# Gelu written back into its PSUM bank and split from there by VectorE, chunk 0's B and C as float32 rows, and the high weights' products first, in a fused scan and two-layer kernel

## The chip, the core and the metric

The kernel runs on one core of a Trainium2 chip. The metric is device time in microseconds (us) of one execution; a run is compared by the median of its executions. The engines have short names here: PE is TensorE, DVE is VectorE, ACT is ScalarE, POOL is GpSimd, and SP is the engine whose queue issues most DMAs.

## What is computed

Three stages stand behind one another. A chunked state-space scan over 768 positions gives y for 4 batches and 8 heads; y, as 3072 rows of 256, goes through two feed-forward layers of width 2048, the first with a sigmoid form of gelu, the second with a clipped form of swish.

```python
cum = np.cumsum(la, axis=-1)                                # la = log(clip(a))
L = np.exp(cum[:, :, :, None] - cum[:, :, None, :]) * causal
CB = np.einsum('bhin,bhjn->bhij', Cc, Bc)
y_intra = np.einsum('bhij,bhjd->bhid', CB * L, xc)
y_inter = np.einsum('bhin,bhnd->bhid', Cc, state) * np.exp(cum)[:, :, :, None]
y[:, :, sl] = y_intra + y_inter                             # and a new state for the next chunk
...
h = x @ w_in;  g = h * (1.0 / (1.0 + np.exp(-1.702 * h)));  x = g @ w_out          # first layer
h = x @ w_in;  g = h * np.clip(h + 3.0, 0.0, 6.0) / 6.0;    out = g @ w_out        # second layer
```

## The kernel before

**Scan.** The 768 positions are cut into 8 chunks c of 96, and each chunk has 4 batches b; the pair is a number q = 4c + b, 0 to 31. For each q and each half g of the heads, `decay` (L374, DVE) makes the decay matrix l by a scan instruction, `s_mm` (L446 for chunk 0, L455 for the others, PE) the products of B and C in a PSUM bank, and their product is the tile gm: by `g_mul` (L458, DVE), or for six of them by a copy on ACT (L461) and `g_pool` (L465, POOL). `y_mm` (L476, PE) multiplies gm by x; `y_out` (L484, ACT) and `y_lo` (L489, DVE) split the result into a high and a low part, the tile xt that the first layer reads. For chunks of q up to 3 the decay row is spread by PE (`a_spread`, L364); later ones load it by DMA (`a_load`).

**Layers.** The 3072 rows are cut into 7 blocks of 384 or 480 columns (`WID`). A unit is one block k, one layer (kind A or B) and one of 16 slices m of the width of 2048: 224 units. A unit is six matmuls of `l1` (L627) into one of two PSUM banks h, the activation, and six of `l2` (L663) into two banks acc. Each factor is a sum of a high and a low part (wh and wl, xt, gh and gl), and the three larger of four products are taken. In a unit of kind A, ACT runs gelu twice out of the bank (L636: to gg in SBUF, and to gh, which rounds), and `g_lo` (L649) on POOL makes gl = gg - gh. In a unit of kind B, ACT, DVE (`hard`, L645) and ACT (L640) make gg and gh, and POOL makes gl.

**Weights.** 32 weight tiles p (16 for each layer) arrive as 64-bit words, 512 KB each, in three buffers raw. Each is decoded: `w_scale` (L293, ACT) into one of two buffers dec, `w_low` (L298, DVE), `w_join` (L302, DVE), `w_top` (L305, ACT) to wh, and `w_bottom` (L311) to wl, on POOL for p under 16 and on DVE from 16 on. The last 9 tiles wl share memory with a tile `late`, which chunk 0's B and C (bcz and cbd) use first.

**Order.** Everything is added to a list with a due time (`key`), an assumed duration, and what it reads and writes; a planner (`Schedule.run`) walks the list with these durations and writes one order for each engine. The engines then run their order strictly, each instruction waiting for semaphores. The order of units is written out: block 0 alone for `LEAD` = 14 slices, then the rest of block 0 between slices of block 1, and so on.

For chunk 0, C is laid out as a block-diagonal tile: `c_block` multiplies it by a mask for each of 8 heads, on ACT (five) and POOL (three), and `s_mm` then makes one matmul of 128 x 448 for each q and g. Chunks 1 to 3 (`ROWS`) use 16 partition rows of float32 for each head instead, and eight matmuls of 16 x 112 for each q.

Of the kernel before, what the change touches and what calls it, by code (L numbers as in the profile page):

```python
# [36 lines left out]
LEAD = 14  # L37
# [5 lines left out]
LOWP = lambda p: False  # L43
TOPA = lambda p: True
# [163 lines left out]
def ssd_moe_kernel(ctx: ExitStack, tc: tile.TileContext, xs, aa, bc, bcz_d, bc0, wu, pat, idn, out):  # L208
# [4 lines left out]
    add = sch.add  # L213

# [19 lines left out]
    bcz = late[:, 0:2 * NB * E].rearrange("p (s b e) -> p s b e", s=2, b=NB)  # L234
    cbd = late[:, 2 * NB * E:10 * NB * E].rearrange("p (h b e) -> p h b e", h=NH, b=NB)
# [36 lines left out]
    mm = lambda k: max(0.1733, WID[k] / 2400 + 0.0025)  # L272
# [31 lines left out]
    def w_top(p, act):  # L304
        (nc.scalar.copy if act else nc.vector.tensor_copy)(w_hi[p], B_(f"dec:{p}").bitcast(F32))  # L305
# [472 lines left out]
```

## Time and profile before

| | |
|---|---|
| runs | median 622.89 us of 3 (621.64 to 623.63) |
| the profiled execution | 621.37 us, of it a span of 619.6 us from first to last instruction |
| busy share of the span | PE 97%, ACT 49%, POOL 53%, DVE 44% |
| granted TensorE clock | 0.993 over the span |
| first matmul of the layers | 23.54 us after the span's start |

The profiled execution is 1.5 us under the median of the runs. The parts of the prediction are worked out inside the profiled execution. A busy share is a mean over the whole span; the stretches differ.

### The profile page before, as it was taken

How to read it: one execution, taken by the hardware profiler on the slowest of the kernel's cores; microseconds unless marked ns; L12 is line 12 of the kernel's file. 1: busy time of each engine (PE TensorE's matmuls, PEld its weight loads, DVE VectorE, ACT ScalarE, POOL GpSimd, SP SyncE). 2: the span in 40 equal slices, each digit the busy share in tenths (PEclk: the TensorE clock that was granted, in tenths of full speed). 3: DMA queues.
4: the chain of work that ended last, by engine and by line, in shares of the span. 5: the costliest groups of instructions: out<-in, count | busy, mean ns of one | idle time of the engine just before them, and what ended most of it. 6: DMA issues, size and time to landing. Idle time of an engine off the chain costs nothing.

```text
span 619.6 us, 9459 instructions
## 1 busy us (share of the span) xinstructions
PE 600.7 (97%) x3580; PEld 527.5 (85%) x3580; DVE 273.6 (44%) x370; ACT 303.9 (49%) x629; POOL 327.3 (53%) x275
## 2 busy tenths in 40 slices
PE   9697799999999999999999999999999999999997
PEld 6575698889999899888888888888888899988997
DVE  6799996655751665412533414523103210032222
ACT  5555665566554454434544336444335444454453
POOL 5699984345475553434843447443344445444452
PEclk9799999999999999999999999999999999999999
DMA  4966553335113492340604404403000000000000
GB/s 145 248 189 197 166 196 109 119 110 175 50 52 107 122 264 78 90 138 1 169 2 129 129 2 122 139 1 118 0 2 1 0 17 15 2 1 1 33 0 27
DMA packets 45918, 53.69 MB, mean 87 GB/s; under 512 B 26176, under 2 KB 37296, under 8 KB 45872
## 3 DMA queue, kind: packets, MB, share of 16 engines
q1 hardware_dynamic: 45600, 52.97, 29.2%
q8 instruction: 28, 0.46, 0.3%
q14 instruction: 18, 0.15, 0.1%
q10 hardware_dynamic: 272, 0.12, 0.1%
HBM read 42.01 MB, written 10.60 MB: 85 GB/s over the span
## 4 chain that ended last, share of the span: by engine, by line
PE 89%; DVE 7%; DMA 1%; issue 1%; ACT 1%; POOL 0%; ACTq 0%; DVEq 0%; POOLq 0%; SPq 0%
PE h L627 43%; PE acc L663 42%; DVE l L374 3%; PE s L455 2%; DVE dec L302 2%; DVE raw L298 1%; PE y L476 1%; DVE gm L458 1%; PE s L476 1%; DMA raw<-in_wu 1%; DMA pat_sb<-in_pat 1%; PE acc L455 0%; DVE xt L489 0%; POOL wl L311 0%; ACT dec L293 0%
## 5 line engine op out<-in xcount | busy, mean ns | idle before, releaser
L649 POOL TENSOR_TENSOR gl<-gg,gh 128x384 fp32r<-128x384 f32 (+1 forms) x223 | 270.3, 1215 | 269.8 <-ACT gh L640 120.1
L627 PE MATMUL h<-xt,wh 128*128 128x480 f32 (+1 forms) x896 | 290.6, 367 | 2.1 <-DVE xt L489 1.8
L627 PEld LDWEIGHTS h<-xt,wh 128*128 128x128 f32 x896 | 168.2, 189 | 21.1 <-issue 2.2
L645 DVE SCALAR_TENSOR_TENSOR gg<-gg,h 128x480 f32<-128x480 f32 (+1 forms) x112 | 68.3, 610 | 229.2 <-ACT gg L638 228.9
L663 PE MATMUL acc<-gh,wh 128*128 128x384 f32 (+1 forms) x448 | 161.8, 361 | 0.0
L663 PE MATMUL acc<-gl,wh 128*128 128x384 f32 (+1 forms) x448 | 128.1, 362 | 0.0
L627 PE MATMUL h<-xt,wl 128*128 128x480 f32 (+1 forms) x322 | 117.8, 366 | 5.9 <-POOL wl L311 5.9
L663 PE MATMUL acc<-gh,wl 128*128 128x480 f32 (+1 forms) x322 | 117.9, 366 | 0.0
L636 ACT ACTIVATE gg<-h 128x480 f32<-128x480 f32 (+1 forms) x112 | 59.9, 537 | 111.2 <-PE h L627 102.8
L638 ACT ACTIVATE gg<-h 128x480 f32<-128x480 f32 (+1 forms) x112 | 60.2, 538 | 78.4 <-PE h L627 72.6
L640 ACT CAST gh<-gg 128x480 fp32r<-128x480 f32 (+1 forms) x112 | 62.6, 559 | 66.1 <-DVE gg L645 66.0
L663 PEld LDWEIGHTS acc<-gh,wh 128*128 128x128 f32 x448 | 84.1, 188 | 7.0
L663 PEld LDWEIGHTS acc<-gl,wh 128*128 128x128 f32 x448 | 82.8, 188 | 8.5 <-POOL gl L649 0.4
L374 DVE TENSOR_TENSOR_SCAN l<-l,pat_sb 112x448 f32<-112x448 f32 x56 | 80.4, 1462 | 5.5 <-DMA l<-acl_d 5.4
L627 PEld LDWEIGHTS h<-xt,wl 128*128 128x128 f32 x322 | 61.2, 190 | 12.4 <-POOL wl L311 7.6
L663 PEld LDWEIGHTS acc<-gh,wl 128*128 128x128 f32 x322 | 60.4, 188 | 7.4 <-issue 2.1
L636 ACT ACTIVATE gh<-h 128x480 fp32r<-128x480 f32 (+1 forms) x112 | 59.7, 533 | 11.5 <-PE h L627 11.5
L663 PE MATMUL acc<-gh,w_late 128*128 128x480 f32 (+1 forms) x126 | 45.8, 364 | 0.0
L627 PE MATMUL h<-xt,w_late 128*128 128x480 f32 (+1 forms) x126 | 45.6, 362 | 0.0
L458 DVE TENSOR_TENSOR gm<-s,l 112x448 f32<-112x448 f32 x28 | 17.3, 618 | 45.5 <-PE s L455 38.2
L302 DVE SCALAR_TENSOR_TENSOR dec<-dec,raw 128x512 uint32<-128x512 uint32 x32 | 33.6, 1049 | 2.4 <-ACT dec L293 0.3
L305 ACT CAST wh<-dec 128x512 fp32r<-128x512 f32 x32 | 19.8, 621 | 20.8 <-DVE dec L302 20.7
(60 smaller groups left out, 384.2 us busy)
## 6 DMA issues: line engine op xcount, KB each, us to landing
raw<-in_wu SPq DMA_DIRECT2D x32, 512.0 KB, 4.8
l<-acl_d SPq DMA_DIRECT2D x28, 392.0 KB, 4.8
st<-scr SPq DMA_DIRECT2D x8, 896.0 KB, 5.5
scr<-tsplit SPq DMA_DIRECT2D x32, 168.0 KB, 3.0
xs<-in_xs SPq DMA_DIRECT2D x8, 384.0 KB, 6.1
out<-gg SPq DMA_DIRECT2D x10, 192.0 KB, 2.0
scr<-tsplit SPq DMA_DIRECT2D x16, 112.0 KB, 2.2
raw<-in_bc SPq DMA_DIRECT2D x4, 384.0 KB, 5.5
```

Of the source, the lines that this page charges most:

```text
L302: nc.vector.scalar_tensor_tensor(t, t, 3, B_(f"raw:{p}")[:, :, 0], ALU.logical_shift_left, ALU.bitwise_or)
L305: (nc.scalar.copy if act else nc.vector.tensor_copy)(w_hi[p], B_(f"dec:{p}").bitcast(F32))
L374: nc.vector.tensor_tensor_scan(t, a, pat_sb, 0.0, ALU.mult, ALU.add)
L455: nc.tensor.matmul(out=ps[:, k, :], lhsT=l, rhs=r, start=True, stop=True)
L458: nc.vector.tensor_tensor(out=B_(f"gm:{q}.{g}"), in0=s_bank(q, g), in1=B_(f"l:{q}")[:, 4 * g:4 * g + 4], op=ALU.mult)
L627: nc.tensor.matmul(out=ps, lhsT=w[p][:, 128 * j:128 * j + 128], rhs=x[:, xp, j, 0:n], start=(i == 0), stop=(i == 5))
L636: nc.scalar.activation(g, ps, AF.Gelu_apprx_sigmoid)
L638: nc.scalar.activation(g, ps, AF.Relu, bias=3.0)
L640: nc.scalar.copy(g, B_(f"gg:{u}")[:, 0:n])
L645: nc.vector.scalar_tensor_tensor(out=g, in0=g, scalar=6.0, in1=B_(f"h:{u}")[:, 0:n], op0=ALU.min, op1=ALU.mult)
L649: e.tensor_tensor(out=B_(f"gl:{u}")[:, 0:n], in0=B_(f"gg:{u}")[:, 0:n], in1=B_(f"gh:{u}")[:, 0:n].bitcast(F32), op=ALU.subtract)
L663: nc.tensor.matmul(out=acc[d], lhsT=w[p][:, 256 + 128 * d:384 + 128 * d], rhs=g, start=(m == 0 and d not in seen), stop=(m == NM - 1 and d ...
```

## The change

- **Gelu.** In units of kind A, ACT writes gelu back into the PSUM bank h, then copies the bank to gh, and DVE makes gl out of the bank and gh. POOL has `g_lo` only for kind B. (`GLV` is now true for all units.)
- **Weights.** `w_bottom` runs on POOL for all 32 tiles.
- **Chunk 0.** `ROWS` now has chunk 0 too: B and C come as rows of float32 by eight DMAs of 56 KB, four of them on ACT's queue, and `c_block` is gone. The rows of chunks 0 to 2 lie in two buffers inside `late`, which also holds a fourth buffer for l (for q = 3).
- **The first DMAs.** The clipped decay factors (acl) take a buffer gg and no longer one of the three raw; pat is issued ahead of idn.
- **Order of products.** `l1` is two pieces: four matmuls with wh, and then two with wl, which alone wait for wl.
- **Planner.** `LEAD` is 12, the assumed durations are new, and an operation on DVE marked `port` is lengthened where it overlaps one on POOL, and the reverse.

```diff
-LEAD = 14
+LEAD = 12
-BOTV = lambda p: p >= 16
-GLV = lambda u, n: u == n - 1
+BOT = lambda p: "POOL"
+GLV = lambda u: True
-CBE = ["ACT", "ACT", "ACT", "POOL", "ACT", "POOL", "ACT", "POOL"]
-ROWS = (1, 2, 3)
+ROWS = (0, 1, 2, 3)
...
+            if o["port"]:
+                other = "DVE" if e == "POOL" else "POOL"
+                o["dur"] += (0.45 if e == "POOL" else 0.6) * max(0.0, min(port[other] - t, o["dur"]))
+                port[e] = t + o["dur"]
...
-    bcz = late[:, 0:2 * NB * E].rearrange("p (s b e) -> p s b e", s=2, b=NB)
-    cbd = late[:, 2 * NB * E:10 * NB * E].rearrange("p (h b e) -> p h b e", h=NH, b=NB)
+    r16_b = [late[:, 16 * E * i:16 * E * i + 16 * E] for i in range(2)]
+    lx_b = [late[0:E, 32 * E:40 * E].rearrange("p (h e) -> p h e", h=NH)]
...
-    add("ACT", 0.1, -90, consts, 0, w=["idn"], kb=20)
-    add("ACT", 0.1, -90, consts, 1, w=["pat"], kb=100)
+    add("ACT", 0.1, -91, consts, 1, w=["pat"], kb=100)
+    add("ACT", 0.1, -90, consts, 0, w=["idn"], kb=20, after=0.05)
...
-    add("SP", 0.4, -80, a_all, new=["raw:acl"], kb=115)
+    add("SP", 0.4, -80, a_all, new=["gg:acl"], kb=115)
...
+        elif c == 0:
+            src = bcz_d[s][64 * g:64 * g + 64].rearrange("(k n) (j p) e -> n p j k e", k=4, p=2)[:, i // 2]
+            eng.dma_start(out=t[:, s].rearrange("n (j k) e -> n j k e", j=2), in_=src)
...
-    def l1(u):
+    def l1(u, lo):
...
-        seq = [(w_hi, 1, 0), (w_lo, 0, 0), (w_hi, 1, 1), (w_lo, 0, 1), (w_hi, 0, 0), (w_hi, 0, 1)]
+        for w, xp, j in ((w_lo, 0, 0), (w_lo, 0, 1)) if lo else ((w_hi, 1, 0), (w_hi, 1, 1), (w_hi, 0, 0), (w_hi, 0, 1)):
...
+        elif kind == "A" and part == 0:
+            nc.scalar.activation(ps, ps, AF.Gelu_apprx_sigmoid)
...
+            nc.scalar.copy(B_(f"gh:{u}")[:, 0:n], ps if kind == "A" else B_(f"gg:{u}")[:, 0:n])
...
+        g = B_(f"{'h' if order[u][0] == 'A' and GLV(u) else 'gg'}:{u}")[:, 0:n]
+        e.tensor_tensor(out=B_(f"gl:{u}")[:, 0:n], in0=g, in1=B_(f"gh:{u}")[:, 0:n].bitcast(F32),
...
+        add("PE", 4 * mm(k), t, l1, u, False, r=W[:1] + [xname(kind, k)] + parts[kind, k], new=[f"h:{u}"])
+        add("PE", 2 * mm(k), t - 50, l1, u, True, r=W[1:] + [xname(kind, k)], w=[f"h:{u}"])
```

What stands in DVE's order when block 0 begins, before the change (raw and dec are weight tiles, l a decay matrix, gm its product with the bank s or acc):

```order
L298 TENSOR_SCALAR raw0_129<-raw0_129 128x512
L302 SCALAR_TENSOR_TENSOR dec1_133<-dec1_133,raw0_129 128x512
L374 SCALAR_TENSOR_TENSOR l1_135<-l1_135,pat_sb_68 112x448 x2
L298 TENSOR_SCALAR raw2_131<-raw2_131 128x512
L302 SCALAR_TENSOR_TENSOR dec0_132<-dec0_132,raw2_131 128x512
L298 TENSOR_SCALAR raw1_130<-raw1_130 128x512
L302 SCALAR_TENSOR_TENSOR dec1_133<-dec1_133,raw1_130 128x512
L374 SCALAR_TENSOR_TENSOR l2_136<-l2_136,pat_sb_68 112x448 x2
```

and after it, at the same place (L387 is now `decay`, L305 `w_low`, L309 `w_join`, L640 `g_lo`):

```order
L387 SCALAR_TENSOR_TENSOR l0_134<-l0_134,pat_sb_68 112x448
L305 TENSOR_SCALAR raw2_131<-raw2_131 128x512
L309 SCALAR_TENSOR_TENSOR dec0_132<-dec0_132,raw2_131 128x512
L640 TENSOR_TENSOR gl0_152<-h1_159,gh0_149 128x384
L305 TENSOR_SCALAR raw0_129<-raw0_129 128x512
L309 SCALAR_TENSOR_TENSOR dec1_133<-dec1_133,raw0_129 128x512
L640 TENSOR_TENSOR gl1_153<-h0_158,gh1_150 128x384
L387 SCALAR_TENSOR_TENSOR l0_134<-l0_134,pat_sb_68 112x448
L387 SCALAR_TENSOR_TENSOR l1_135<-l1_135,pat_sb_68 112x448
```

One `g_lo` now stands behind each join, and reads the bank h; before, none stood on DVE here. On POOL, the same stretch held one tile wl and one gl by turns before the change:

```order
L311 TENSOR_TENSOR wl2_107<-dec0_132,wh2_75 128x512
L649 TENSOR_TENSOR gl0_152<-gg0_147,gh0_149 128x384
L311 TENSOR_TENSOR wl3_108<-dec1_133,wh3_76 128x512
L649 TENSOR_TENSOR gl1_153<-gg1_148,gh1_150 128x384
L649 TENSOR_TENSOR gl2_154<-gg0_147,gh2_151 128x384
L311 TENSOR_TENSOR wl4_109<-dec0_132,wh4_77 128x512
```

and holds tiles wl alone after it, with a product gm for the scan (L468) here and there:

```order
L318 TENSOR_TENSOR wl2_107<-dec0_132,wh2_75 128x512
L318 TENSOR_TENSOR wl3_108<-dec1_133,wh3_76 128x512
L318 TENSOR_TENSOR wl4_109<-dec0_132,wh4_77 128x512
L468 TENSOR_TENSOR gm1_138<-gm1_138,l0_134 112x448
L318 TENSOR_TENSOR wl5_110<-dec1_133,wh5_78 128x512
```

On SP, the queue of the first DMAs before the change, in which the third weight tile stands behind acl's store and takes a buffer that the first tile had:

```order
L383 DMA late_128<-in_bcz 128x448 x2
L377 DMA xs0_141<-in_xs 96x1024
L288 DMA raw1_130<-in_wu 128x1024
L288 DMA raw2_131<-in_wu 128x1024
L356 DMA acl_d_155<-raw0_129 128x224
L288 DMA raw1_130<-in_wu 128x1024
```

and after it, where the first three tiles have a buffer each:

```order
L433 DMA late_128<-in_bcz 16x8x112 x4
L390 DMA xs0_141<-in_xs 96x1024
L295 DMA raw0_129<-in_wu 128x1024
L367 DMA acl_d_155<-gg0_147 128x224
L295 DMA raw1_130<-in_wu 128x1024
L295 DMA raw2_131<-in_wu 128x1024
```

The third weight tile no longer waits for a buffer.

## Rows read from the trace of the kernel before

**Rows 1.** Busy time by stretch: engines' busy us (instructions), granted clock, DMA share, GB/s.

```profile
0.00:23.50 23.50, 18.06 (x124) 11.37 (x124) 17.21 (x25) 11.82 (x26) 13.45 (x19) 0.94 0.61 196
23.50:27.50 4.00, 3.96 (x12) 3.96 (x13) 2.55 (x4) 1.63 (x4) 1.34 (x2) 0.50 1.04 266
...
30.00:71.40 41.40, 32.30 (x256) 26.26 (x255) 40.32 (x40) 22.61 (x52) 38.10 (x26) 1.00 0.62 181
100.00:600.00 500.00, 499.70 (x2888) 441.71 (x2887) 182.96 (x266) 240.67 (x490) 242.97 (x210) 1.00 0.24 70
```

**Rows 2.** PE's waits from 0 to 80 us: who waited for whom, us, times, longest.

```profile
PE h L627 <- POOL wl L311: 5.9, 6, 1.4
```

**Rows 3.** The chain of waits: start us, us, what.

```profile
15.27 5.10 DMA raw<-in_wu
...
23.54 5.32 PE h L627 x18
...
590.08 2.10 PE h L627 x12
```

**Rows 4.** Timeline of DVE, 0 to 110 us: start us, us, instruction.

```profile
5.14 3.05 DVE L374 TENSOR_TENSOR_SCAN l<-acc,pat_sb 112x448 f32<-112x448 f32 x3 [1.86 <-DMA pat_sb<-in_pat]
...
18.14 1.08 DVE L374 TENSOR_TENSOR_SCAN l<-acc,pat_sb 112x448 f32<-112x448 f32 x1
...
45.73 0.42 DVE L298 TENSOR_SCALAR raw<-raw 128x512 uint32<-128x512 uint32 x1
46.25 0.69 DVE L302 SCALAR_TENSOR_TENSOR dec<-dec,raw 128x512 uint32<-128x512 uint32 x1
46.86 2.15 DVE L374 TENSOR_TENSOR_SCAN l<-l,pat_sb 112x448 f32<-112x448 f32 x1
...
49.45 0.34 DVE L489 TENSOR_TENSOR xt<-y,xt 128x192 fp32r<-128x192 f32 x1
...
66.26 1.78 DVE L302 SCALAR_TENSOR_TENSOR dec<-dec,raw 128x512 uint32<-128x512 uint32 x1
...
103.73 2.06 DVE L374 TENSOR_TENSOR_SCAN l<-l,pat_sb 112x448 f32<-112x448 f32 x2
```

**Rows 5.** Groups of instructions, 23.5 to 71.4 us: busy us, mean ns | idle before, releaser.

```profile
L311 POOL TENSOR_TENSOR wl<-dec,wh 128x512 fp32r<-128x512 f32 x12 | 20.4, 1698 | 4.9 <-ACT wh L305 4.9
L649 POOL TENSOR_TENSOR gl<-gg,gh 128x384 fp32r<-128x384 f32 x13 | 19.9, 1532 | 2.9 <-ACT gh L636 2.7 <-POOL wl L311 0.3
L374 DVE TENSOR_TENSOR_SCAN l<-l,pat_sb 112x448 f32<-112x448 f32 x10 | 17.8, 1794 | 1.3 <-DMA l<-acl_d 1.3
L302 DVE SCALAR_TENSOR_TENSOR dec<-dec,raw 128x512 uint32<-128x512 uint32 x12 | 17.2, 1429 | 1.4 <-ACT dec L293 0.3
L298 DVE TENSOR_SCALAR raw<-raw 128x512 uint32<-128x512 uint32 x12 | 7.2, 601 | 0.0
```

**Rows 6.** Timeline of POOL: start us, us, instruction.

```profile
14.44 1.74 POOL L465 TENSOR_TENSOR gm<-gm,l 112x448 f32<-112x448 f32 x1 [0.93 <-ACT gm L461]
...
54.91 1.26 POOL L311 TENSOR_TENSOR wl<-dec,wh 128x512 fp32r<-128x512 f32 x1
...
101.70 1.00 POOL L649 TENSOR_TENSOR gl<-gg,gh 128x384 fp32r<-128x384 f32 x1 [1.39 <-PE acc L663]
```

**Rows 7.** Groups by shape over the whole span, columns as in rows 5.

```profile
L636 ACT ACTIVATE gg<-h 128x384 f32<-128x384 f32 x48 | 23.5, 490 | 36.1 <-PE h L627 28.8 <-POOL gl L649 7.0 <-DMA out<-gg 0.3
L458 DVE TENSOR_TENSOR gm<-acc,l 112x448 f32<-112x448 f32 x16 | 9.8, 614 | 0.0
L671 DVE TENSOR_TENSOR xt<-acc,xt 128x384 fp32r<-128x384 f32 x6 | 3.1, 551 | 1.1 <-ACT xt L673 1.1
```

**Rows 8.** DMA issues: KB each, median us to landing.

```profile
raw<-in_wu SPq DMA_DIRECT2D x32, 512.0 KB, 4.8
...
st<-in_bc SPq DMA_DIRECT2D x32, 24.0 KB, 2.0
late<-in_bcz SPq DMA_DIRECT2D x2, 224.0 KB, 3.7
```

More of the change, by code (lines that the diff above doesn't have):

```diff
@@ L139, in run @@
         ends = {}
+        port = {"DVE": 0.0, "POOL": 0.0}
         pipe = 0.0
@@ L213, in ssd_moe_kernel @@
     add = sch.add
+    ENG = {"ACT": nc.scalar, "DVE": nc.vector, "POOL": nc.gpsimd}
     const = pool("const")
@@ L271, in ssd_moe_kernel @@
     NU = len(order)
[L272 removed]
+    mm = lambda k: 0.000452 * WID[k]
     tu, t = [], START
@@ L443, in s_mm @@
                 ps = s_bank(q, g)
-                if c == 0:
-                    if k == 0:
-                        nc.tensor.matmul(out=ps, lhsT=bcz[:, 0, b], rhs=cbd[:, 4 * g:4 * g + 4, b], start=True, stop=True)
-                    continue
                 if c in ROWS:
@@ L503, in ssd_moe_kernel @@
     sname, yname, rows = {}, {}, {}
-    add("SP", 0.4, -80, a_all, new=["raw:acl"], kb=115)
-    add("DVE", 0.35, -80, a_clip, w=["raw:acl"])
-    add("SP", 0.4, -70, bcz_load, 1, w=["bcz1"], kb=230)
-    add("SP", 0.4, -69, bcz_load, 0, w=["bcz0"], kb=230)
-    add("SP", 0.4, -1, a_store, r=["raw:acl"], w=["acl_d"], kb=115)
-    for h in range(NH):
-        e = CBE[h]
-        add(e, {"ACT": 0.55, "POOL": 0.95, "DVE": 0.4}[e], -50 + h, c_block, h, e, r=["bcz1", "idn"], w=[f"cbd{h}"])
+    add("SP", 0.4, -80, a_all, new=["gg:acl"], kb=115)
+    add("DVE", 0.35, -80, a_clip, w=["gg:acl"])
+    add("SP", 0.4, -1, a_store, r=["gg:acl"], w=["acl_d"], kb=115)
     add("POOL", 0.4, -40, zero_xs, new=["xs:0"])
@@ L571, in ssd_moe_kernel @@
         if c in ROWS:
-            add("PE", 0.9, t + 1, s_mm, q, (0, 1), r=[f"st:{c}"] + rows[c], new=[sname[q, 0], sname[q, 1]])
+            add("PE", 0.9, t + 1, s_mm, q, (0, 1), r=[rname(c)] + rows[c] + ["late"] * (c < 3), new=[sname[q, 0], sname[q, 1]])
         for g in range(2):
-            if c == 0:
-                add("PE", 0.85, t + 1 + 0.1 * g, s_mm, q, (g,), r=["bcz0"] + [f"cbd{h}" for h in range(4 * g, 4 * g + 4)], w=["late"], new=[sname[q, g]])
-            elif c not in ROWS:
+            if c not in ROWS:
                 add("PE", 0.3, t + 1 + 0.1 * g, s_mm, q, (g,), r=[f"st:{c}.{b // 2}"], new=[sname[q, g]])
@@ L624, in l1 @@
         ps = B_(f"h:{u}")[:, 0:n]
[L625 to L626 removed]
+        for w, xp, j in ((w_lo, 0, 0), (w_lo, 0, 1)) if lo else ((w_hi, 1, 0), (w_hi, 1, 1), (w_hi, 0, 0), (w_hi, 0, 1)):
             nc.tensor.matmul(out=ps, lhsT=w[p][:, 128 * j:128 * j + 128], rhs=x[:, xp, j, 0:n],
[L628 removed]
+                             start=not lo and (xp, j) == (1, 0), stop=lo and j == 1)
     def act(u, part):
@@ L633, in act @@
         ps = B_(f"h:{u}")[:, 0:n]
-        g = (B_(f"gh:{u}") if part else B_(f"gg:{u}"))[:, 0:n]
-        if kind == "A":
+        if kind == "A" and not GLV(u):
+            g = B_(f"{'gh' if part else 'gg'}:{u}")[:, 0:n]
             nc.scalar.activation(g, ps, AF.Gelu_apprx_sigmoid)
+        elif kind == "A" and part == 0:
+            nc.scalar.activation(ps, ps, AF.Gelu_apprx_sigmoid)
         elif part == 0:
-            nc.scalar.activation(g, ps, AF.Relu, bias=3.0)
+            nc.scalar.activation(B_(f"gg:{u}")[:, 0:n], ps, AF.Relu, bias=3.0)
         else:
-            nc.scalar.copy(g, B_(f"gg:{u}")[:, 0:n])
+            nc.scalar.copy(B_(f"gh:{u}")[:, 0:n], ps if kind == "A" else B_(f"gg:{u}")[:, 0:n])
     def hard(u):
```

155 lines of the change are left out of this document (74 added, 81 removed).

## The prediction

> **What bounds the kernel now.** I read the busy time by stretch first [rows 1], with PE's column. From 100 to 600 us PE is busy 499.70 of 500 us: whatever the other engines do there costs nothing, and nothing can be won there by making them lighter. Only the first 71 us are different. Until 23.5 us the layers have not begun. From 30 to 71.4 us PE is busy 32.30 of 41.40 us, so 9.1 us are idle, while DVE is busy 40.32 and POOL 38.10. So there are two things to win at the front and no others: an earlier first layer matmul, and the 9.1 us.
>
> PE's waits say what it idles for [rows 2]: of these, 5.9 us in six waits are for a tile wl from POOL, the longest 1.4. The chain of waits [rows 3] shows what comes before: at 15.27 us it goes for 5.10 us through the load of a weight tile, and the layers begin at 23.54.
>
> DVE and POOL are full in this stretch partly because they hinder each other. Where POOL is quiet, a scan takes 1.03 us (two in 2.06), a join 0.69, a low 0.42; a scan beside POOL's work takes 2.15 [rows 4]. The means from 23.5 to 71.4 us are 1.794, 1.429 and 0.601 us [rows 5]. For 10 scans, 12 joins and 12 lows that is 7.6 + 8.9 + 2.2 = 18.7 us more than alone. POOL's wl takes 1.698 against 1.26 alone, its gl 1.532 against 1.00 [rows 5, 6]. An operation of DVE that reads a PSUM bank does not show this: gm from the bank acc takes 0.614 us on the mean of 16 [rows 7].
>
> **Gelu in the bank.** POOL loses a gl per unit of block 0, 1.00 us alone; DVE gets one. The trace has its like in the split of a drained bank, PSUM and SBUF in and SBUF out at 128x384: 0.551 us [rows 7]. If it were drawn out like a scan (1.794/1.03), it would be 0.96; I take 0.55, since the gm out of PSUM is not drawn out. ACT's second pass is a copy and no longer a second gelu, and the first writes PSUM, which no row shows. Its price lies between nothing and one more pass of 0.490 [rows 7]; I take no difference, and ACT has room for the upper end (22.61 us busy of 41.40).
>
> The Trainium skill ("SBUF — State Buffer", Who interferes with whom) says that a VectorE instruction with two SBUF inputs contends with a GpSimd instruction that reads SBUF, by a lock, and that one with at most one SBUF input does not. The trace agrees on both halves (2.15 against 0.614). By that rule the new g_lo stays at 0.55; if it were 0.96, the ten of them in the ledger below would cost 4.1 us more.
>
> **The ledger of DVE.** I count DVE's order from the end of the scan of chunk 0 to the join of weight tile 12. Before: 9 scans, 10 pairs of low and join, 6 gm, 4 xt. By distance from start to start a low is 0.52 and a join 0.61 [rows 4], so 9 x 1.03 + 10 x 1.13 + 6 x 0.61 + 4 x 0.34 = 25.6 us. It took from 23.5 to 68.0 us (66.26 + 1.78) [rows 4], 44.5 us: 1.3 of the rest were a wait for a DMA [rows 5], so 17.6 were contention. After: 8 scans, 11 pairs, 10 gl, 5 gm, 3 xt: 8.2 + 12.4 + 5.5 + 3.1 + 1.0 = 30.2 us. POOL's work alone in this stretch was about 12 wl, 13 gl and 2 products gm: 15.1 + 13.0 + 2.3 = 30.4 us, and is 17.4 without gl. If contention shrinks in proportion (17.6 of 30.4, or 0.58 us on DVE for each us of POOL), it is 10.1, and the stretch is 40.3 us. The gain is 4.2 us, with bounds from a loss of 3.3 (contention as before, 47.8 us) to 9.1 (PE never waits). So the change moves as much to DVE as it takes from it in contention, and a little more comes out.
>
> **The start.** The first scan began at 5.14 us, on landing of pat [rows 4]; pat goes first in its queue, which I put at 0.4 us. DVE's order then has eight scans (three take 3.05 [rows 4]), three gm, one low, and two xt up to the end of the last scan of q = 3: 8.1 + 1.8 + 0.4 + 0.7 = 11.0 us, so 15.7. Before, this scan ended at 19.22 (18.14 + 1.08 [rows 4]), since two lows and two joins stood ahead. Behind it come POOL's gm (1.74 [rows 6]), y_mm, y_out and y_lo, and on DVE two joins and a low. It took 4.3 us to the first layer matmul before; 3.5 now, since the cast of the third weight tile no longer stands ahead of y_out on ACT. So about 19.2 us, which wins 4.3. Bounds: 18.3, if the scan ends as early as it may, and 21.0, if both joins meet POOL at the mean of 1.43 and the rows of chunk 0 land late. These rows come by eight DMAs of 56 KB; the nearest land 2.0 us (24 KB) and 3.7 us (224 KB) after issue [rows 8], and they stand second in their queues, so they are there when the first scan ends, and nothing like `c_block` follows them. The third weight tile, with its own buffer, is issued with the first ones; with 4.8 us to landing [rows 8] and two tiles ahead of it I put it at 12 us, where before it landed at 20.4 (15.27 + 5.10 [rows 3]).
>
> **What else costs nothing.** wl of tiles 16 to 31 moves from DVE to POOL, which loses a gl per unit of kind A in exchange; PE is fully busy there, and this cover holds as long as it is. The order of products changes no count of matmuls. It lets four of six matmuls start without wl, so a wait on wl of up to 0.7 us is hidden; the six waits [rows 2] would be halved. `LEAD` 12 spreads tiles 12 to 15 over twice the units, so the last of the stalls (1.4 us [rows 2]) should mostly go: I take 0.7. At the clock I take nothing: from 23.5 to 27.5 us the granted clock was 0.50, the lower level of 1.2 GHz [rows 1], and 12 matmuls took 4.0 us where they later take 2.10 [rows 3]. PE has a gap ahead of the layers after the change too. If it stays at 2.4 GHz, 1.9 us more are won.
>
> **The sum.** 4.3 + 4.2 + 0.7 = 9.2 us off 621.37 gives 612.2 us for a profiled execution. That one lies 1.5 us under the median of the runs, so the median should be about 613.5.
>
> **Rivals.** *PE bound from its first unit.* The reduced contention and the lighter order free PE of all 9.1 us of idling, and the start comes at 18.9: 4.6 + 9.1 = 13.7, or 609 us; with the clock held, 607. For it: the weights' due times and DVE's ledger (40.3 us) lie within 2 us of PE's own work for these 12 units (25.2 us of matmuls, and some 12 for the scan and the slow clock). Against: three engines and a queue run in strict order, and each late link holds all.
>
> *DVE gains nothing.* DVE holds 5.5 us of gl in front of its joins, and waits in order for ACT's copy (POOL waited 2.7 us for gh [rows 5]). If that eats the 4.2 us, only the start remains: 2.5 to 4.3, so 618.5 to 620.4. A late weight does the same: a raw buffer is loaded again only when its tile is joined, and the load takes 4.8 us [rows 8], with ACT and DVE about 7 for three tiles; it would have to take 11 to set the pace of 3.6 us per tile in the ledger. At the far end, DVE would lose the whole of POOL's 17.4 us: the stretch would be 47.6 us, 3.1 of the start's 4.3 us would be lost again, and the time about 621, no change. That is what the lock of the Trainium skill (the page above) gives if DVE is always the loser. The trace bears out 0.58 us of each, so this end has a small chance.
>
> *Slower: the bank is held too long.* A bank h used to be free after two passes of ACT (0.98 us). Now it is held for gelu, copy, and DVE's gl: 0.49 + 0.49 + 0.55 and three handovers of about 0.1, 1.85 us. PE needs it again after an l2, an l1 and an l2, three times 1.05 us (half of 2.10 [rows 3]), so there are 1.3 us of slack for a scan that stands in front of gl (1.03). In every unit of kind A, also where PE is now never idle, two scans in a row would pass it. With 112 such units, a mean wait of 0.10 us in each takes back the 9.2 us and 1.9 more; 0.15 us would give 630. Against it: DVE is busy 37% from 100 to 600 us (182.96 of 500 [rows 1]), and a scan is needed only twice for each of the 19 remaining q.
>
> **How the numbers follow.** Two kernels of this kind can be told apart from 0.3%, 1.9 us. My forecast, with its own range of 609.5 to 617.5, has a chance of 0.57, PE bound from the first unit (under 609.5) 0.15, only the start (617.5 to 621) 0.17, no change 0.05, slower 0.06. So faster 0.89. The range from 607.5 to 619.5 takes in most of both neighbours and leaves about 0.18 out.
>
> **What would show it.** The first layer matmul near 19.2 us, with no weight load in the chain ahead of it. From there to about 62 us, PE idle for 3 to 6 us and no longer 9; DVE still over 90% busy, but with scans nearer 1.4 than 1.79 us, and gl on DVE at 0.55. wl alone at about 1.5. After 65 us PE without waits, and matmuls of `l1` not waiting for DVE's gl. It is wrong if PE waits for DVE in the units of kind A after 100 us, if the scans stay at 1.8 us, or if the layers begin after 21 us.

## The result, and the profile after

The changed kernel takes 614.63 us at the median of 4 runs (614.59 to 615.93), against 622.26 of the kernel before beside it (621.63 to 623.63). The ratio is 0.9879, with an interval of 0.9856 to 0.9903. The profiled execution is the slowest of the four, 615.93 us with a span of 614.1; its distance to the profiled execution of before is 5.4 us, where the medians differ by 7.6. Two executions far off all the others (833.85 us at a granted clock of 0.655, of the kernel with matmuls in the gap ahead of the layers, and 981.64 at 0.556, of the kernel before) are left out below.

Busy time by stretch, over three stretches of [rows 1] and the ledger's own (from the first layer matmul to the join of weight tile 12); columns as there:

```profile
0.00:23.50 23.50, 19.91 (x180) 15.45 (x181) 16.86 (x26) 8.36 (x20) 10.80 (x17) 0.93 0.70 185
30.00:71.40 41.40, 36.38 (x278) 30.84 (x279) 36.81 (x53) 25.49 (x55) 18.82 (x12) 0.92 0.73 213
100.00:600.00 500.00, 500.00 (x2884) 442.74 (x2883) 223.17 (x339) 248.21 (x492) 160.90 (x136) 1.00 0.24 68
20.90:61.84 40.94, 34.94 (x244) 29.48 (x245) 37.23 (x51) 25.30 (x53) 22.15 (x14) 0.92 0.79 217
```

From 100 to 600 us PE is busy all the time, as before; DVE has risen from 182.96 to 223.17 us and nothing shows of it. From 30 to 71.4 us PE is busy 36.38 us where it was 32.30, at a granted clock of 0.92 where it was 1.00, and POOL has fallen from 38.10 to 18.82.

PE from the first layer matmul to 80 us, in the kernel before and in the kernel after:

```profile
23.54:80.00 56.46, 47.37 (x337) 40.59 (x338) 53.55 (x53) 31.05 (x70) 50.49 (x33) 0.96 0.67 184
20.96:80.00 59.04, 53.10 (x361) 46.63 (x362) 53.94 (x73) 36.96 (x78) 28.90 (x18) 0.92 0.73 204
```

It idles for 9.1 us before and for 5.9 after. Over the whole span PE is busy as long as before (600.75 and 600.97 us), so the 5.5 us between the two spans are idling: 18.9 us before, 13.1 after. Of the difference, 1.9 us lie ahead of the first layer matmul, 3.2 between it and 80 us.

PE's waits from 0 to 80 us:

```profile
PE acc L654 <- DVE gl L640: 2.0, 1, 2.0
PE h L615 <- POOL wl L318: 1.8, 4, 0.7
...
PE h L615 <- ACT wh L312: 1.0, 1, 1.0
```

The waits for wl are 1.8 us and no longer 5.9 [rows 2]. New is one wait of 2.0 us for DVE's gl. The same view from 65 us on is empty: there PE waits for no bank, neither for gelu nor for gl.

The first layer matmul on PE, three scans and the join of weight tile 12 on DVE (timelines of the two engines):

```profile
20.96 1.65 PE L615 MATMUL h<-xt,wh 128*128 128x384 f32 x4 [1.50 <-DVE xt L492]
```

```profile
5.68 1.09 DVE L387 TENSOR_TENSOR_SCAN l<-acc,pat_sb 112x448 f32<-112x448 f32 x1 [2.01 <-PE acc L375]
7.05 1.09 DVE L387 TENSOR_TENSOR_SCAN l<-acc,pat_sb 112x448 f32<-112x448 f32 x1 [0.29 <-PE acc L375]
...
16.53 1.08 DVE L387 TENSOR_TENSOR_SCAN late<-acc,pat_sb 112x448 f32<-112x448 f32 x1
...
60.52 1.32 DVE L309 SCALAR_TENSOR_TENSOR dec<-dec,raw 128x512 uint32<-128x512 uint32 x1
```

The layers begin at 20.96 us, 2.6 earlier than before. The first scan waited for PE's spread of the decay factors (L375), not for pat.

The chain of waits (each step is what the next one waited for), in the kernel before:

```profile
30.04 1.38 DVE dec L302
...
66.26 1.79 DVE dec L302
70.06 1.25 POOL wl L311
```

and in the kernel after:

```profile
3.84 3.17 PE acc L375 x8
...
21.09 8.26 DMA late<-in_bc
29.42 5.28 DMA raw<-in_wu
...
60.00 1.31 POOL wl L318
```

Before, it stays on DVE from 30.0 to 68 us. After, it runs through PE's own matmuls up to 17.3 us, with no weight load ahead of the layers, then through two loads from 21.1 to 34.7 us, is on DVE from 45.7 to 59.3, and leaves the weights at 61.35, where PE takes over.

Groups of instructions from 23.5 to 71.4 us, columns as in [rows 5]:

```profile
L318 POOL TENSOR_TENSOR wl<-dec,wh 128x512 fp32r<-128x512 f32 x13 | 21.5, 1663 | 19.6 <-ACT wh L312 19.6
L387 DVE TENSOR_TENSOR_SCAN l<-l,pat_sb 112x448 f32<-112x448 f32 x8 | 14.5, 1818 | 0.0
L309 DVE SCALAR_TENSOR_TENSOR dec<-dec,raw 128x512 uint32<-128x512 uint32 x13 | 14.1, 1084 | 1.1 <-ACT dec L300 0.4
L640 DVE TENSOR_TENSOR gl<-h,gh 128x384 fp32r<-128x384 f32 x14 | 7.7, 547 | 2.3 <-ACT gh L630 2.3
L305 DVE TENSOR_SCALAR raw<-raw 128x512 uint32<-128x512 uint32 x13 | 5.3, 410 | 0.7 <-DMA raw<-in_wu 0.7
```

A scan is as long as before (1.818 us, 1.794 before), a join is shorter (1.084 for 1.429), and a low is as short as alone (0.410 for 0.601 before). gl out of the bank takes 0.547 us on DVE beside POOL's work.

### The profile page after: what moved, and what is told of

Same layout as the page of the kernel before. It is cut to its first block, busy times and chain, and to the rows that moved or that the text cites. A ratio compares the mean times of both kernels' runs of the same rounds, so it can differ in the third digit from the quotient of the medians.

```text
span 614.1 us, 9456 instructions
## 1 busy us (share of the span) xinstructions
PE 601.0 (98%) x3628; PEld 530.6 (86%) x3628; DVE 310.4 (51%) x466; ACT 310.3 (51%) x624; POOL 207.1 (34%) x176
## 4 chain that ended last, share of the span: by engine, by line
PE 93%; DMA 2%; DVE 2%; ACT 1%; issue 1%; POOL 0%; SPq 0%; ACTq 0%; DVEq 0%; POOLq 0%
PE h L615 43%; PE acc L654 43%; PE s L458 2%; PE y L479 2%; PE acc L375 1%; DMA late<-in_bc 1%; PE s L479 1%; DMA raw<-in_wu 1%; DVE dec L309 1%; DVE l L387 1%; PE h L458 1%; PE acc L458 0%; PE y L335 0%; DVE gl L640 0%; DVE raw L305 0%
## 5 line engine op out<-in xcount | busy, mean ns | idle before, releaser
L640 POOL TENSOR_TENSOR gl<-gg,gh 128x480 fp32r<-128x480 f32 (+1 forms) x111 | 133.2, 1202 | 315.8 <-ACT gh L630 285.8
L615 PE MATMUL h<-xt,wh 128*128 128x480 f32 (+1 forms) x896 | 220.2, 368 | 2.5 <-DVE xt L492 1.5
L615 PEld LDWEIGHTS h<-xt,wh 128*128 128x128 f32 x896 | 162.9, 190 | 21.1 <-issue 3.5
L640 DVE TENSOR_TENSOR gl<-h,gh 128x480 fp32r<-128x480 f32 (+1 forms) x112 | 68.5, 611 | 121.5 <-ACT gh L630 99.6
L626 ACT ACTIVATE h<-h 128x480 f32<-128x480 f32 (+1 forms) x112 | 58.4, 521 | 111.2 <-PE h L615 111.0
L628 ACT ACTIVATE gg<-h 128x480 f32<-128x480 f32 (+1 forms) x112 | 60.3, 538 | 78.3 <-PE h L615 75.9
L615 PE MATMUL h<-xt,wl 128*128 128x480 f32 (+1 forms) x322 | 91.5, 365 | 1.8 <-POOL wl L318 1.8
L387 DVE TENSOR_TENSOR_SCAN l<-l,pat_sb 112x448 f32<-112x448 f32 x56 | 78.8, 1421 | 3.2 <-DMA l<-acl_d 3.1
L630 ACT CAST gh<-h 128x480 fp32r<-128x480 f32 (+1 forms) x112 | 58.9, 526 | 4.4
L318 POOL TENSOR_TENSOR wl<-dec,wh 128x512 fp32r<-128x512 f32 x23 | 36.1, 1582 | 58.2 <-ACT wh L312 58.2
L615 PE MATMUL h<-xt,w_late 128*128 128x480 f32 (+1 forms) x126 | 35.2, 360 | 0.0
L309 DVE SCALAR_TENSOR_TENSOR dec<-dec,raw 128x512 uint32<-128x512 uint32 x32 | 28.9, 903 | 2.9 <-ACT dec L300 1.2
```

Source lines behind the costliest of these rows:

```text
L309: nc.vector.scalar_tensor_tensor(t, t, 3, B_(f"raw:{p}")[:, :, 0], ALU.logical_shift_left, ALU.bitwise_or)
L318: e.tensor_tensor(out=w_lo[p], in0=B_(f"dec:{p}").bitcast(F32), in1=w_hi[p].bitcast(F32), op=ALU.subtract)
L387: nc.vector.tensor_tensor_scan(t, a, pat_sb, 0.0, ALU.mult, ALU.add)
L615: nc.tensor.matmul(out=ps, lhsT=w[p][:, 128 * j:128 * j + 128], rhs=x[:, xp, j, 0:n], start=not lo and (xp, j) == (1, 0), stop=lo and j == 1)
L626: nc.scalar.activation(ps, ps, AF.Gelu_apprx_sigmoid)
L628: nc.scalar.activation(B_(f"gg:{u}")[:, 0:n], ps, AF.Relu, bias=3.0)
```

## The experiments

All of them change the kernel after, unless said otherwise. The table holds for each the start of the first layer matmul and the end of the join of weight tile 12 in its profiled execution, and the time, with its ratio to the kernel before on the same chip (whose median there was 622.05 to 622.65 us). The intervals are 2 to 6 us wide, so "no difference" means none that they show, and a microsecond can hide in it. An edit that moves work or changes a duration also makes the planner write another order; a run prices both together.

| kernel | `LEAD` | first layer matmul | tile 12 joined | median us | ratio and interval |
|---|---|---|---|---|---|
| before | 14 | 23.54 | 65.49 | 622.26 | |
| after | 12 | 20.96 | 61.84 | 614.63 | 0.9879 (0.9856 to 0.9903) |
| gelu in the bank alone | 14 | 23.20 | 59.08 | 617.24 | 0.9895 (0.9858 to 0.9931) |
| start, planner and order of products alone | 14 | 20.84 | 67.95 | 623.62 | 1.0028 (1.0006 to 1.005) |
| all but gelu in the bank | 12 | 20.26 | 62.31 | 622.33 | 0.9986 (0.9959 to 1.0012) |
| after, `LEAD` 14 | 14 | 20.79 | 59.27 | 615.55 | 0.9885 (0.9861 to 0.991) |
| after, wl of tiles 0 to 15 on DVE | 12 | 20.61 | 62.94 | 617.79 | 0.9916 (0.9883 to 0.9949) |
| after, cheap spreads | 12 | 22.20 | 62.42 | 615.29 | 0.9884 (0.9865 to 0.9902) |

**All but gelu in the bank.**

```diff
-GLV = lambda u: True
+GLV = lambda u: False
```

> The changed kernel with one part undone: units of kind A run gelu twice, to gg and gh in SBUF, and gl is made on POOL again. If the front of the kernel is paced by DVE and its contention with POOL, the pace term is lost: DVE is rid of 11 gl of 0.55 us but POOL's work in the stretch rises from about 17 to 30 us, which at 0.58 us per us costs DVE 7.5; the time rises by 1.5 to 4 us, to 616 to 619, and joins and scans last 0.3 us longer on the mean. If gl on DVE was an even trade and the gain came from the start and the order of products, 614.6 within 1 us.

622.33 us, more than either expectation: nothing is left of the gain. POOL is busy 36.59 of the 40.94 us from 20.9 to 61.84, where it was 22.15. The time goes in several places, and not only up to tile 12. PE waits for wh in six places, and once for ACT's gelu; its largest waits from 0 to 80 us:

```profile
PE h L615 <- ACT wh L312: 3.6, 6, 1.0
PE h L615 <- ACT gg L624: 2.7, 1, 2.7
```

Ahead of the second one, at 69.7 us, DVE sat idle for 5.45 us for a load of l:

```profile
75.11 1.09 DVE L387 TENSOR_TENSOR_SCAN l<-l,pat_sb 112x448 f32<-112x448 f32 x1 [5.45 <-DMA l<-acl_d]
```

The planner has written another order here, so this run does not price gl on POOL by itself; it shows that the other edits together bring nothing without the edit of gelu.

**Gelu in the bank alone**, in the kernel before, for all units of kind A:

```diff
...
-            nc.scalar.activation(g, ps, AF.Gelu_apprx_sigmoid)
+        if kind == "A" and part == 0:
+            nc.scalar.activation(ps, ps, AF.Gelu_apprx_sigmoid)
...
-        if GLV(u, NU):
+        if kind == "A" or u == NU - 1:
...
```

> The kernel before with one part added: gelu written back into the bank and gl made on DVE in units of kind A, everything else (chunk 0, weights' buffers, order of products, LEAD 14, wl on DVE from tile 16) as before. If contention is what it relieves, 2 to 4.5 us faster than before, 618 to 620. If it is an even trade, 622.3 within 1 us. If the bank held longer costs PE in units of kind A, slower than before.

617.24 us, 5 us less than before (a little more than expected), with a start that is 0.3 us earlier. Tile 12 is joined 6.4 us earlier. So this edit has most of the gain, and has it without the others. PE's idling from the first layer matmul to 80 us is 3.7 us here, and 9.6 in the run above.

**The new start alone** of the large parts: gelu twice, gl on POOL, wl of tiles 16 to 31 on DVE and `LEAD` 14, as before. The order of products and the planner's new durations stay changed.

```diff
-GLV = lambda u: True
+GLV = lambda u: False
-BOT = lambda p: "POOL"
+BOT = lambda p: "DVE" if p >= 16 else "POOL"
-LEAD = 12
+LEAD = 14
```

> The changed kernel with gelu twice, gl of all units on GpSimd, wl of tiles 16 to 31 on VectorE and LEAD 14, as before the change: of the large parts only the new start is left. If the start's 2.6 us are won by themselves, about 619.5. Rival: an earlier start alone is eaten by the full VectorE and GpSimd behind it, as where only gl went back to GpSimd (622.3): 621 to 623.

The rival was nearer: 623.62 us, 0.3% more than before. The layers begin 2.7 us earlier, but tile 12 is joined 2.5 us later. PE then waits for the weights, 5.4 us for wh and 1.4 for wl:

```profile
PE h L615 <- ACT wh L312: 5.4, 6, 2.9
```

That is not the whole of it. PE idles for 9.5 us from the first layer matmul to 80 us, where it was 9.1, and for 1.4 from 80 to 600 us, where it was 0.3; over the whole span it idles even a little less than before (18.3 us for 18.9). But it is busy for 603.6 us and no longer 600.8, with a granted clock of 0.91 between the first layer matmul and 80 us, where it was 0.96.

**One piece of l1**, with the products by turns as before:

```diff
-    def l1(u, lo):
+    def l1(u):
...
+        seq = [(w_hi, 1, 0), (w_lo, 0, 0), (w_hi, 1, 1), (w_lo, 0, 1), (w_hi, 0, 0), (w_hi, 0, 1)]
...
```

> The changed kernel with the order of products undone: six matmuls of l1 in one piece, high and low weights by turns. After the change PE still waited 1.8 us in four waits for wl, and two matmuls with wh (about 0.35 us at full clock) more would stand behind each such wait. If these four matmuls hide a wait for wl, 1 to 3 us slower, 616 to 617.5, with PE waiting for wl for 3 to 5 us. If they hide nothing that another link does not take back, 614.6 within 0.7 us.

615.59 us, a ratio of 0.9868 (0.9823 to 0.9914): no difference to the changed kernel that shows. PE's waits for wl are 1.7 us in four places, as in the changed kernel (1.8 in four). The order of products is worth nothing that shows.

**acl in a raw buffer**, as before:

```diff
-        return B_("gg:acl")[:, 0:2 * E]
+        return raw32("raw:acl", 2, E)
...
```

> The changed kernel with the decay factors back in one of the three raw buffers, so that the third weight tile loads only when a buffer comes free. If the load of the third tile set the start of the layers, they begin 1.5 to 3 us later than 20.96 us and the time is 616 to 617.5. If the start is set by chunk 0's own chain (rows landing at 5.5 to 8.3 us, scans, products), the layers begin at 21 us as before and the time is 614.6 within 0.7 us, with at most a short wait at the third unit.

615.03 us, 0.9866 (0.982 to 0.9911): no difference that shows. The layers begin at 20.98 us, so the load of the third weight tile does not set the start.

**wl of the first 16 tiles on DVE**, so that POOL does next to nothing up to 62 us:

```diff
-BOT = lambda p: "POOL"
+BOT = lambda p: "DVE" if p < 16 else "POOL"
```

> The changed kernel with wl of the first 16 weight tiles on VectorE, not GpSimd. If a tile wl on GpSimd costs VectorE about 0.58 us for each of its 1.26 us alone, then 12 of them in the ledger cost VectorE 8.8 us, and as VectorE's own work they cost about as much (12 x 0.73): scans go back to 1.03 us and joins to 0.69, and the ledger stays within 2 us of 40.9; the time is 612.5 to 616. Rival: scans are drawn out by something other than GpSimd and stay near 1.74 us; then VectorE only gets 8.8 us more work and the time is 619 to 623.

The groups from 23.5 to 71.4 us:

```profile
L309 DVE SCALAR_TENSOR_TENSOR dec<-dec,raw 128x512 uint32<-128x512 uint32 x12 | 8.6, 719 | 0.4 <-ACT dec L300 0.3
L387 DVE TENSOR_TENSOR_SCAN l<-l,pat_sb 112x448 f32<-112x448 f32 x8 | 8.5, 1078 | 0.0
L318 DVE TENSOR_TENSOR wl<-dec,wh 128x512 fp32r<-128x512 f32 x12 | 8.3, 691 | 1.4 <-ACT wh L312 1.4
L640 DVE TENSOR_TENSOR gl<-h,gh 128x384 fp32r<-128x384 f32 x14 | 7.7, 552 | 4.0 <-ACT gh L630 4.0
L305 DVE TENSOR_SCALAR raw<-raw 128x512 uint32<-128x512 uint32 x13 | 5.5, 421 | 2.8 <-DMA raw<-in_wu 2.8
```

Scans are back at 1.078 us and joins at 0.719: the drawing out of DVE came from POOL's work. DVE, with 8.3 us more work of its own, is even less busy in the ledger's stretch (33.45 us of 40.94, for 37.23). And yet the time is no shorter: 617.79 us (614.5 to 618.88), above the 612.5 to 616 expected and below the rival's 619, and tile 12 is joined 1.1 us later than in the changed kernel. DVE now waits, 4.0 us for ACT's gh and 2.8 for a weight load, and PE for them (2.4 us for gh, 2.3 for gl at the longest). So in the changed kernel DVE's work is no longer what sets the pace of the weights alone.

**`LEAD` 14:**

```diff
-LEAD = 12
+LEAD = 14
```

> The changed kernel with LEAD back at 14. The prediction put the spread of tiles 12 to 15 at 0.7 us, so it gives 615.3. Rival: GpSimd has room now and the last tiles come in time either way: no difference from 614.6, within 0.5 us.

615.55 us: no difference that can be told apart. Its one profiled execution, 613.69 us, has no wait of PE above 0.7 us behind the start, but eleven short ones for wl and wh that add up to 5.2 us.

**wl of tiles 16 to 31 on DVE**, as before, with the rest of the change:

```diff
-BOT = lambda p: "POOL"
+BOT = lambda p: "DVE" if p >= 16 else "POOL"
```

> The changed kernel with wl of tiles 16 to 31 on VectorE, as before the change. The prediction put this move at nothing, since TensorE never waits there: no difference from 614.6, within 1 us. Rival: VectorE with gl and wl both is late somewhere after 65 us, TensorE waits there, and the time is 616 or more.

614.90 us, 0.9877 (0.9856 to 0.9899): no difference that shows. The cover that the prediction named holds: PE has no waits from 65 us on.

**Cheap spreads.** The decay factors of chunk 0 are spread in one pass of bfloat16:

```diff
-            nc.tensor.matmul(out=..., lhsT=idn_sb[:, j:j + 1].to_broadcast([128, E]),
-                             rhs=f, start=True, stop=True)
+            nc.tensor.matmul(out=..., lhsT=idn_sb.bitcast(BF16)[:, 2 * j + 1:2 * j + 2].to_broadcast([128, E]),
+                             rhs=f.bitcast(BF16).rearrange("p (e t) -> p e t", t=2)[:, :, 1], start=True, stop=True)
```

> The changed kernel in which TensorE's spreading of chunk 0's decay factors takes one pass of bfloat16 instead of float32 (the decay factors of chunk 0 are cut to 8 bits, which is the part of the computation that changes). If these 32 matmuls on TensorE set the time to the first layer matmul, as the waits of VectorE's scans say, the first scan begins about 1 us earlier, the others don't wait, and the first layer matmul comes at 19.2 us or earlier, where the prediction had it, 1.5 to 2 us ahead of the changed kernel; the time falls by as much, to 613. Rival: VectorE's own order sets it, and the first layer matmul stays within 0.5 us of 20.4 to 21.0.

Neither came. The first scan did begin 1.4 us earlier, at 4.25, so the spread had held it:

```profile
4.25 2.07 DVE L387 TENSOR_TENSOR_SCAN l<-acc,pat_sb 112x448 f32<-112x448 f32 x2 [0.73 <-PE acc L375]
```

But the first layer matmul came at 22.20 us, 1.2 later than in the changed kernel, because PE's other matmuls ran slower. Groups of PE from 0 to 22 us, of this kernel:

```profile
L458 PE MATMUL h<-late 16*112 16x112 f32 x64 | 8.0, 407 | 1.4 <-DMA late<-in_bcz 1.4
L375 PE MATMUL acc<-gg,idn_sb 128*112 128x224 bf16 x16 | 3.9, 397 | 0.0
```

and of the kernel after:

```profile
L375 PE MATMUL acc<-gg,idn_sb 128*112 128x224 f32 x32 | 8.5, 418 | 0.0
L458 PE MATMUL h<-late 16*112 16x112 f32 x64 | 4.3, 268 | 0.0
```

The products of the rows take 0.407 us for 0.268. (The granted clock of this stretch prints as 1.00 here; the durations speak against it, and two other executions of this kernel, 614.71 and 614.82 us, have a mean of 0.983 and 0.986, lower than any of the changed kernel.) With 1.2 us lost at the start, tile 12 is joined only 0.6 us later, and the time, 615.29 us, cannot be told from that of the changed kernel. A first layer matmul that is a microsecond later costs nothing that shows here.

**Matmuls in the gap ahead of the layers.** 13 of them, 64 x 256, that nobody needs, in bank h:

```diff
+        if u == 0 and not lo:
+            for _ in range(13):
+                nc.tensor.matmul(out=B_(f"h:{u}")[0:64, 0:256], lhsT=pat_sb[:, 0:64], rhs=pat_sb[:, 0:256], start=True, stop=True)
```

> The changed kernel with 13 matmuls of 64 x 256 that nobody needs in bank h ahead of the first layer matmul, while TensorE waits 1.5 us for xt. If that gap brings the drop to half clock from 20.4 to 23.8 us, the drop is gone and 1.7 us are won: about 613. Rival: the drop comes anyway, from the shorter gaps before it or later in the stretch: 614 to 615, or slower by the length of the extra matmuls.

617.46 us at the median of three executions (614.35 to 617.89), 0.9905 (0.9871 to 0.9939). In the profiled execution the granted clock was still 0.84 from 19 to 23 us and 0.85 from 23 to 30. PE's timeline:

```profile
21.35 2.64 PE L616 MATMUL h<-pat_sb 112*64 112x256 bf16 x13
23.93 1.52 PE L618 MATMUL h<-xt,wh 128*128 128x384 f32 x4
```

The 13 matmuls took 2.64 us, and the layers began at 23.93. Some 2 us of this were lost earlier (the last product of chunk 0 with x starts at 20.23, and at 18.27 in the changed kernel), in a stretch up to 19 us with a clock of 0.91. The two shorter gaps, 0.61 and 0.39 us ahead of the halves of that product, are still there. The rival was right, but since this execution had lost its clock once already (0.57 from 8 to 12 us, where the changed kernel prints 1.00), it is no clean test of the last gap.

**Matmuls in all three gaps** (5 and 4 ahead of the two halves of `y_mm` for q = 3, and 13 as above):

```diff
         for g in range(2):
+            for _ in range((5, 4)[g] if q == 3 else 0):
+                nc.tensor.matmul(out=B_("acc:fill")[0:64, 0:256], lhsT=pat_sb[:, 0:64], rhs=pat_sb[:, 0:256], start=True, stop=True)
             for k in range(4):
...
```

> The changed kernel with matmuls of 64 x 256 that nobody needs in all three of TensorE's gaps ahead of the layers: 5 and 4 ahead of the two halves of the last product of chunk 0 with x, 13 ahead of the first layer matmul. If the drop to half clock at 20 to 24 us comes from these 2.5 us of idling together, it is gone with them, the extra matmuls take about 0.1 us each and fit the gaps, and 1.7 us are won: about 613. Rival: the drop comes anyway, the extra matmuls take 0.2 us each and push the first layer matmul back by 1 to 2 us: 615 to 617.

The clock holds up to 30 us, and the extra matmuls fit the gaps. PE's timeline, and the busy time by stretch, of the slowest execution (617.52 us):

```profile
17.37 0.73 PE L478 MATMUL acc<-pat_sb 112*64 112x256 bf16 x5
...
19.26 1.61 PE L618 MATMUL h<-pat_sb 112*64 112x256 bf16 x13
20.79 0.97 PE L620 MATMUL h<-xt,wh 128*128 128x384 f32 x4
```

```profile
19.00:23.00 4.00, 3.91 (x31) 3.06 (x31) 3.86 (x8) 2.94 (x7) 2.94 (x2) 1.00 0.64 200
23.00:30.00 7.00, 5.09 (x26) 4.36 (x26) 6.89 (x7) 4.30 (x9) 4.02 (x3) 1.00 0.93 170
30.00:62.00 32.00, 27.96 (x203) 23.07 (x201) 26.26 (x38) 18.71 (x40) 14.73 (x9) 0.84 0.64 205
```

But the time is 614.31 us, 0.9868 (0.9846 to 0.9889), no difference to the changed kernel. With full clock from 19 to 30 us PE is idle in 1.9 us of 23 to 30, of them 1.07, 0.23 and 0.70 in waits for wl: it only comes sooner to a weight tile that is not there. The four other executions, with a mean granted clock of 0.996 to 0.999, took 613.46 to 615.02 us; this one has 0.988 over its span and 0.84 from 30 to 62 us.

**The same with `LEAD` 14:**

```diff
-LEAD = 12
+LEAD = 14
```

> The changed kernel with the extra matmuls in the three gaps ahead of the layers and with LEAD 14, whose profiled execution alone had no wait of TensorE over 0.7 us behind the start and no later drop of the clock. If drops behind such waits are what separates the executions, this one keeps full clock from 4 us on in most executions and takes 612 to 613.5. Rival: the weight tiles set the pace of the first 65 us whatever the clock is there, and waits of TensorE bring a drop later: 614 to 616, as the changed kernel.

616.05 us (614.68 to 617.83), 0.991 (0.9894 to 0.9925), with a mean granted clock of 0.993 to 1.000. Five of the six executions are above the 612 to 613.5 expected by more than 1.5 us, and the median is at the upper end of the rival's range. The profiled one (614.68) has a clock of 1.00 up to 30 us and 0.95 from 30 to 62; the one with 1.000 over its whole span took 615.27. So full clock did not shorten the time there. No version here beats the changed kernel by more than the scatter.

## Why the prediction was right, step by step

The forecast of 613.5 us is 1.1 from the 614.63 measured. The main part of its cause is shown from both sides: gelu in the bank brings 5 us alone, and without it the rest brings nothing. That POOL's work draws DVE out is shown too, since POOL off altogether brings the scans back to 1.078 us. That the time was won by less drawing out, and not by POOL's lighter load as such (busy 38.10 of 41.40 us before), is argued: no run took work off POOL without also easing DVE. The chain of waits speaks for DVE, on which it stays from 30.0 to 68 us before.

That the number came so near is partly luck. Of the three terms, 4.3 for the start, 4.2 for the ledger and 0.7 for `LEAD`, the first measured 2.6, the second 1.1, and the third cannot be told from nothing.

**Contention: right.** By the means alone (1.03 for a scan, 0.69 for a join), DVE's excess from 23.5 to 71.4 us was 18.7 us; after, it is 8 x 0.79 + 13 x 0.39 = 11.4, or 0.61 of it. The prediction had 0.57 (17.4 of 30.4). But it is divided otherwise than it said: the scans stay long and the joins and lows get short. By the prediction's own sign, that it is wrong if the scans stay at 1.8 us, it fails here (1.818); the sign was badly chosen, since it is the sum that shrank. wl took 1.663 us and not about 1.5. How the loss is shared goes with the order: with `LEAD` 14 a scan takes 1.441 us and a wl 1.808.

**The ledger before: read off a wrong row.** The prediction took the join at 66.26 us for tile 12's. Counted in DVE's order, it is tile 13's, and tile 12's is this one in the timeline of the kernel before:

```profile
64.06 1.43 DVE L302 SCALAR_TENSOR_TENSOR dec<-dec,raw 128x512 uint32<-128x512 uint32 x1
```

The ledger before was 42.0 us and not 44.5. After, it was forecast at 40.3 us and took 40.9 (20.96 to 61.84), so its gain is 1.1 us and not 4.2. That 40.3 and 40.9 agree is luck. With the right row the same sum has 42.0 - 25.6 - 1.3 = 15.1 us of contention before, 15.1 x 17.4/30.4 = 8.6 after, and a ledger of 30.2 + 8.6 = 38.8. Measured, DVE's work alone is 30.2 us as counted (8 scans, 11 pairs, 10 gl, 5 gm, 3 xt), its waits are 3.1 (2.0 for ACT's gh, the rest for a weight load and for ACT's `w_scale`), and 7.6 are left for contention. So contention shrank a little more than in proportion, and the waits in order, which the sum put at nothing and only the rival "DVE gains nothing" named, took 3.1 us.

What the prediction gave to the ledger shows in PE's idling from the first layer matmul to 80 us, which fell by 3.2 us (9.1 to 5.9). In every run with gl on DVE it is 3.7 to 7.8 us, in the three kernels with gl on POOL 9.1 to 9.6. The waits for single tiles tell less: for wl and wh together they are 2.8 us after, but 5.2 with `LEAD` 14, which is no slower that shows. PE's busy time from 30 to 71.4 us tells less too. It rose by 4.1 us, but with only 6 layer matmuls and 16 small ones more, at a lower clock.

**The start: too large, and not worth what it was priced at.** 20.96 us, not 19.2; 2.6 us, not 4.3. The step that failed is the first scan at 4.7 us on landing of pat. It waited for PE's spread until 5.68, and the scans waited for the next spreads as well (0.29 us and others), so the last scan ended at 17.61 and not at 15.7; from there to the first layer matmul it took 3.35 us, near the 3.5 forecast. The prediction had counted DVE's order there and not PE's, which was busy 17.36 of the 20.96 us and holds the chain of waits up to 17.3. Its first eight spreads took 3.19 us and the next eight 1.77. More important, the term was counted as time won. The start without gelu in the bank wins nothing (623.62), and 1.2 us later costs nothing that shows (615.29). Against gelu in the bank alone, the changed kernel idles 1.2 us less ahead of the first layer matmul and 2.2 us more from there to 80 us: a unit that begins earlier waits for its tile.

What the start is worth behind gelu in the bank stays open all the same. The other edits together are worth 2.6 us there (617.24 to 614.63), with ratios whose intervals overlap. The order of products, acl's buffer, `LEAD` and wl of the later tiles could each be undone alone without a difference that shows; chunk 0's rows with pat first, which make the start, and the planner's new durations were not undone alone. And the kernel with matmuls in the one gap, whose layers began 3.0 us later, took 617.46 us (614.35 to 617.89).

**wl of tiles 16 to 31, `LEAD`, order of products.** Each was undone alone and each is worth nothing that can be told. For `LEAD` the prediction had 0.7; undoing it cost 0.9 by the medians and 0.4 by the ratios, within the scatter.

**The clock: nothing, for another reason.** After the change the granted clock is low in three places, at the lower of its two levels (1.2 of 2.4 GHz) for most of each stretch. Busy time by stretch of the kernel after:

```profile
20.00:24.00 4.00, 3.04 (x10) 3.00 (x10) 3.90 (x6) 2.50 (x7) 3.71 (x2) 0.57 0.84 211
37.00:41.00 4.00, 3.70 (x18) 3.05 (x18) 2.85 (x7) 2.08 (x5) 1.35 (x2) 0.57 0.82 282
61.00:65.00 4.00, 3.77 (x26) 3.01 (x25) 3.90 (x6) 2.04 (x4) 2.02 (x2) 0.57 0.77 233
```

Before, it was 1.00 in the second and third of these stretches. Ahead of each fall PE had waited: 0.61, 0.39 and 1.50 us, then 1.14 for POOL's gm, then 1.98 for DVE's gl. Filling the gaps ahead of the layers took away the first fall, and no time was won. What the third one costs, behind which PE waits no more, no run shows apart.

**The rivals.** PE bound from its first unit did not come: 5 us of idling remain from 30 to 71.4 us. Too long a hold of the bank did not come either: PE has no wait after 65 us. "DVE gains nothing" came in part: its waits, 2.0 of 3.1 us for ACT's copy, ate most of what the ledger was to win.

The Trainium skill ("SBUF — State Buffer", Who interferes with whom) has it that a VectorE instruction with at most one SBUF input, outside the modes that use both ports, does not contend with GpSimd. The trace agrees: gl, out of the bank and gh, takes 0.547 us beside POOL's work and 0.552 without it. The prediction left the exception out; the low, with one SBUF input, is drawn out in the kernel before (0.601 us on the mean, 0.42 alone), and no run shows which mode it runs in.

What stays open is which link sets the pace of the weights after the change. DVE alone does not, since less contention brought nothing in the run with wl on DVE. In the one trace the chain of waits goes through two loads from 21.1 to 34.7 us and through DVE from 45.7 to 59.3; no run took either away alone.

## What to carry to other kernels

When two engines hinder each other, price the move of an operation by what both lose, and look for a form of it that does not meet the other engine: here a second operand out of PSUM instead of SBUF. An earlier start is only worth what the slowest chain behind it lets through; undo it alone, beside the other edits, before counting it. When a ledger is kept between two rows of a timeline, count the instructions between them in the engine's order, since a row one off is a step's whole gain.

## What was not expected of the hardware

DVE and POOL together lose about what POOL's work takes alone. Before, from 23.5 to 71.4 us, DVE's excess is 18.7 us and POOL's 12 x 0.44 + 13 x 0.53 = 12.2, together 30.9 [rows 5, 6], with 12 x 1.26 + 13 x 1.00 = 28.1 us of POOL's work alone. After, it is 11.4 + 13 x 0.40 = 16.6, with 13 x 1.26 = 16.4. In the other kernels with wl on POOL the same sum, with the two gm on POOL counted at 1.13 us alone, is 0.79 to 1.05 of POOL's work alone, and DVE bears 0.46 to 0.73 of that work. The exclusive lock of the Trainium skill ("SBUF — State Buffer", Who interferes with whom) would give this, with now one engine, now the other as the one that waits; that is worked out from means and was not tested apart.

A PE with less to do can be a slower one. With the spreads in one pass instead of float32's, PE stayed slow up to the layers: the products of the rows took 0.407 us where they take 0.268 in the changed kernel. In the run with extra matmuls in all three gaps, the opposite, the clock was 1.00 from 19 to 30 us, where it is 0.57 from 20 to 24 in the changed kernel. That is one trace each. In the first of them PE had also stood idle for 0.89 and 0.53 us between 4.6 and 6.7 us, until rows of chunk 0 landed, so that the lighter work itself is the reason is not shown.
